# A fused attention and expert kernel: the first slots of its tail are put in another order

## The chip, the cores and the metric

The kernel runs on one core of a Trainium2 chip. The metric is device time in microseconds, the median of several runs; lower is better. Before the change it is 1239.16 us (three runs, 1238.08 to 1239.4). The five engines are named as the profile names them: PE (matrix products), DVE (vector), ACT (scalar, and a queue of DMA issues of its own), POOL (GpSimd, which also issues gathers and scatters) and SP (issues most DMAs).

## The reference, cut to what matters

```python
def _attn_ref(q, k, v):                      # 8 batches, 8 heads, 576 rows, 64 columns
    scores = scale * np.matmul(q, k.transpose(0, 1, 3, 2))
    kth = np.partition(scores, -32, axis=-1)[..., -32:-31]
    scores = np.where(scores >= kth, scores, -1e9)       # the 32 largest of each row stay
    attn = np.exp(scores - max); attn = attn / (sum(attn) + 1e-9)
    return np.matmul(attn, v)
def _moe_ref(x, w_gate, w_output_gate, w1, w2):          # x: 4608 rows of 512; 8 experts
    e_idx = np.argmax(x @ w_gate, axis=1)                # one expert for each row
    gate_w = softmax(x @ w_gate) at e_idx
    eom = 1.0 / (1.0 + np.exp(-(x @ w_output_gate)))
    for e in range(8):
        mask = e_idx == e
        h = np.maximum(x[mask] @ w1[e], 0.0)             # 512 to 1024
        out[mask] = gate_w * eom[mask, e] * (h @ w2[e])  # 1024 to 512
    return out
```

Everything is float32. The rows of `x` are the attention's output, so which expert a row goes to is known only when its attention is done.

## The kernel before

The attention runs over 36 tiles of 128 rows. 144 steps (a tile and a pair of heads each) form scores, find the 32nd largest, weigh and multiply with the values. Each finished tile is written to DRAM (`x_rows`), and gates its 128 rows. Tiles are collected in 12 groups. When a group's last tile is gated, `group_route` (L548) computes on DVE each row's expert and its place, and POOL scatters one list entry for each row into `ids` in DRAM (L612). Then a slot table is made (`slot_table`, L641): which expert's weights a slot of 128 rows takes and where its list begins.

A slot is the work for 128 rows of one expert: its list is read from `ids` by a DMA in ACT's queue (`fetch_id`, L743), its rows are gathered by POOL (`xg`, L759), turned on PE (L769) and copied by ACT (`xs`, L772); `up` is 64 products with the first weights `w1t` (L780), in two halves; `down` follows with the second weights `w2t`; `put` (L798) copies and scatters the result. Weights are 2 MB each, fetched by SP, with two buffers each.

During the attention, slots are woven between its steps (`heavy`). The tail is what follows the last step. Three slots belong to the last group but one: call them A, B and C. A is under way as the tail begins and its `down` pieces run in `while heavy`. B and C, and nine slots D to L of the last group, run in `slots_in_turn`. There `down` is done in three passes of faster products: `split` has ACT copy half of a slot's second weights to `w2h` (L1084) and DVE subtract that from them to `w2l` (L1085); `up_split` makes `hth` on ACT (L1092) and `htl` on DVE (L1093); `down_split` multiplies (L1102), 12 products for each half. `w2h`, `w2l`, `hth` and `htl` lie in a pool (`mp2`) that takes the memory of the attention's keys and scores.

Between these pieces `background` gates the last tile, routes the last group and issues its scatters; `last_table` makes the last slot table on DVE (L658 to L699), from which SP and ACT read weights' and lists' places (`last_slots`). `unsettled` (L189 to L203) is a check over all thresholds: eight operations on DVE, a small product on PE (L198) and four more on DVE, the last of which writes `more`; at the program's end all engines read `more` and jump past a spare path.

The program's order is the order in which this code issues instructions: each engine's queue is filled in that order, and nothing reorders it.

Of the kernel before, what the change touches and what calls it, by code (L numbers as in the profile page):

```python
# [10 lines left out]
F32 = mybir.dt.float32  # L11
F32R = mybir.dt.float32r
# [3 lines left out]
AF = mybir.ActivationFunctionType  # L16
ALU = mybir.AluOpType
# [6 lines left out]
P = 128  # L24
# [18 lines left out]
def tile_topk_attention_moe(  # L43
# [11 lines left out]
    nc = tc.nc  # L55
# [6 lines left out]
    NF = FF // P  # L62
# [120 lines left out]
    def unsettled(cp, pp):  # L183

        lo = cp.tile([P, 2], F32, name="lo")

        far = cp.tile([P, NTT * H], F32, name="gap")
        gap = far.rearrange("p (i a) -> p i a", a=2)
        nc.vector.tensor_scalar(gap, NEAR[:, :, :, 1], 1.0 + 2.0 ** -19, None, op0=ALU.mult)  # L189
        nc.vector.tensor_tensor(gap, gap, NEAR[:, :, :, 0], op=ALU.subtract)  # L190
        nc.vector.tensor_reduce(lo[:, 0:1], far, axis=AX.X, op=ALU.max)
        nc.vector.tensor_scalar(far, KTH, -1.0, None, op0=ALU.mult)
        nc.vector.tensor_tensor(far, far, KTH, op=ALU.max)
        nc.vector.tensor_reduce(lo[:, 1:2], far, axis=AX.X, op=ALU.min)
        nc.vector.tensor_scalar(lo[:, 0:1], lo[:, 0:1], 0.0, None, op0=ALU.is_ge)
        nc.vector.tensor_scalar(lo[:, 1:2], lo[:, 1:2], TINY, None, op0=ALU.is_le)
        bad = pp.tile([P, 2, P], F32, name="po")
        nc.tensor.matmul(bad[:1, 0, :2], ones[:, 0:1], lo, start=True, stop=True)  # L198
        total = cp.tile([1, 1], F32, name="total")
        nc.vector.tensor_reduce(total, bad[:1, 0, :2], axis=AX.X, op=ALU.add)  # L200
        nc.vector.tensor_copy(flag, total)
        nc.vector.tensor_tensor(total, total, over, op=ALU.add)
        nc.vector.tensor_copy(more, total)  # L203

    def run(exact, stack):
# [48 lines left out]
        def fill(n=1, single=False):  # L254
            for _ in range(n):
                if urgent:
                    urgent.popleft()()
                elif small and not (single and getattr(small[0], "two", False)) and small[0]() is not False:
                    small.popleft()
# [462 lines left out]
        W, G, XS, HT, PY = {}, {}, {}, {}, {}  # L722
        gathers = [0]
        tail = [False]

        def expert(g, k):
            if g in FIXED:
# [8 lines left out]
            W.setdefault(s, [None, None])[0] = a  # L736

        def fetch_w2(s, g, k, rows):
            b = mp.tile([P, NF, DM], F32, name="w2t", bufs=2)
            nc.sync.dma_start(b, w2[expert(g, k)].rearrange("o (c p) f -> p (o c) f", p=P))  # L740
            W.setdefault(s, [None, None])[1] = b

# [22 lines left out]
        def turn(s, pool, name):  # L765
            x = G[s][1]
            px = pool.tile([P, NC, P], F32, name=name)
            for c in range(NC):
                nc.tensor.transpose(px[:, c, :], x[:, c * P:(c + 1) * P], ident)  # L769
            def ev():  # L770
                XS[s] = mp.tile([P, NC, P], F32, name="xs", bufs=2)
                nc.scalar.activation(XS[s], px, AF.Copy)  # L772
            return ev

        def up_products(s, f0):
            w = W[s][0]
            ph = pools["p"].tile([P, 4, P], F32, name="pm")
            for f in range(f0, f0 + 4):
                for c in range(NC):
                    nc.tensor.matmul(ph[:, f - f0, :], w[:, c, f * P:(f + 1) * P], XS[s][:, c, :],  # L780
                                     start=(c == 0), stop=(c == NC - 1))
            return ph
# [44 lines left out]
        def ahead(what, f, n, after=None, lag=0):  # L827

            while had[what] < min(len(order), cur[0] + n):
                s = had[what]  # L830
                if after and when.get((after, s), clock[0]) + lag > clock[0]:
                    return
                f(s, *order[s])
                when[what, s] = clock[0]
                had[what] += 1
# [15 lines left out]
        def fetch_ahead():  # L851

            for what, f in (("w1", fetch_w1), ("w2", fetch_w2)):
                ahead(what, f, 1 if heavy else 2)
# [25 lines left out]
        def heavy_piece():  # L880

            return heavy.popleft()() if heavy else None
# [172 lines left out]
        def background():  # L1055
            step[0] += 1
            extra = side_start()
            if extra:
                extra(ps_t.tile([P, 4, P], F32, name="pst"))()
                side_use()  # L1060
            fill(60)
            run_slow(1e9, ("table", "done", "ids", "x", "out"))
# [2 lines left out]
        HL = {}  # L1065
        small_end = lambda: small.extend(slot_table(NGRP - 1, True) + [lambda: queue_slots(NGRP - 1, usual, N)])

        def slots_in_turn():

            def prepare(n):  # L1070
                ahead("id", fetch_id, min(n + 2, listed[0] - cur[0]))
                ahead("x", fetch_x, n + 1)
                ahead("w1", fetch_w1, n)
                ahead("w2", fetch_w2, n)

            def turned(n):
                ahead("turn", lambda s, *_: turn(s, pools["p"], "pm")(), min(n, had["x"] - cur[0]))

            def split(s, part):

                w = W[s][1][:, 4 * part:4 * part + 4]
                hi, lo = [pools["w"].tile([P, 4, DM], F32R, name=n, bufs=3) for n in ("w2h", "w2l")]
                HL[s, part] = hi, lo
                nc.scalar.activation(hi, w, AF.Copy)  # L1084
                nc.vector.tensor_tensor(lo, w, hi.bitcast(F32), op=ALU.subtract)  # L1085

            def up_split(s, f0):
                if f0 == 0:
                    HT[s] = [pools["w"].tile([P, NF, P], F32R, name=n, bufs=1) for n in ("hth", "htl")]
                ph = up_products(s, f0)  # L1090
                hi, lo = [x[:, f0:f0 + 4, :] for x in HT[s]]
                nc.scalar.activation(hi, ph, AF.Relu)  # L1092
                nc.vector.scalar_tensor_tensor(lo, ph, 0.0, hi.bitcast(F32), op0=ALU.max, op1=ALU.subtract)  # L1093

            def down_split(s, f0):
                if f0 == 0:
                    PY[s] = pools["p"].tile([P, DM], F32, name="pm")
                hh, hl = HT[s]
                wh, wl = HL.pop((s, f0 // 4))
                for f in range(f0, f0 + 4):  # L1100
                    for k, (h, w) in enumerate(((hh, wh), (hh, wl), (hl, wh))):
                        nc.tensor.matmul(PY[s], h[:, f, :], w[:, f - f0, :], start=(f == 0 and k == 0),  # L1102
                                         stop=(f == NF - 1 and k == 2))

            def splitted(s, part):
                if s < min(len(order), had["w2"]) and (s, part) not in HL:
                    split(s, part)
            while cur[0] < len(order):
                s = cur[0]
                prepare(1)  # L1110
                turned(1)
                prepare(2)
                splitted(s, 0)
                splitted(s, 1)
                ahead("w2", fetch_w2, 3)
                for f0 in (0, 4):
                    up_split(s, f0)
                    yield
                ahead("w1", fetch_w1, 3)
                for part in range(2):  # L1120
                    splitted(s + 1, part)
                    down_split(s, 4 * part)
                    if part == 0:
                        turned(2)
                    yield
                put(s)
                cur[0] += 1

        while heavy:
            background()  # L1130
            fetch_ahead()
            ev = heavy_piece()
            if ev:
                ev()
        usual = min(NLAST, USUAL)
        background()
        def last_table():
            nonlocal small_end
            if small_end and not (urgent or small or side):
                small_end()  # L1140
                small_end = None
                fill(60)
                ahead("id", fetch_id, min(3, listed[0] - cur[0]))
                ahead("x", fetch_x, 2)
        for n, _ in enumerate(slots_in_turn()):
            background()
            if n:
                last_table()
        while urgent or small or side or small_end:
            background()  # L1150
            last_table()
        if not exact:
            unsettled(st, ps_o)
        for _ in slots_in_turn():
            pass

        def extra_slots():

# [79 lines left out]
```

## Time and profile before

| what | value |
|---|---|
| median of three runs | 1239.16 us |
| the profiled execution's own time | 1241.63 us |
| its span in the profile | 1239.8 us |
| PE, DVE, ACT, POOL busy | 93%, 87%, 77%, 58% of the span |
| 1080.30 to 1231.29 us | slots B to L in the tail |
| granted clock of PE | 0.98 of full speed over the span |

Busy time of PE is modelled from the pipelined products, so it does not say that PE runs at its peak. In a timeline, a number in square brackets is the time that the engine had stood idle before that row, and what ended it. Times are microseconds from the span's start, unless a column says ns.

### The profile page before, as it was taken

To read this page: it belongs to the slowest core of one execution; us is meant where nothing else is said; L and a number is where in the kernel's file an instruction comes from. 1 tells how busy PE (TensorE), PEld (TensorE's weight loads), DVE (VectorE), ACT (ScalarE), POOL (GpSimd) and SP (SyncE) were. 2 spreads that over 40 slices of the span, in tenths; PEclk is the share of its full clock that TensorE was granted. 3 is DMA by queue.
4 is the path that set the end of the run, shared out by engine and by line. 5 is a ranking of instruction groups with operands and counts; after the bars stand their busy time and mean duration, and the time that the engine had idled before them with its cause. 6 is when DMAs were issued, how large, how long until landed. Compare 5 with 4: busy or idle time off the path is not lost.

```text
span 1239.8 us, 31208 instructions
## 1 busy us (share of the span) xinstructions
PE 1158.6 (93%) x9946; PEld 892.9 (72%) x9946; DVE 1074.5 (87%) x6148; ACT 948.5 (77%) x1892; POOL 713.7 (58%) x1191
## 2 busy tenths in 40 slices
PE   5777777899999999999999999999999999989997
PEld 3555555777777777777777777777777777779996
DVE  6999999899999999999999999999999998254443
ACT  5999998888788888887887878888888787334542
POOL 6667667555446584867567675477765486223121
PEclk7999998899999999999999999999999999999999
DMA  6301245077445629297555755566365426499990
GB/s 141 71 19 35 56 165 190 28 217 267 167 160 162 185 97 323 74 297 254 187 178 177 236 182 190 178 208 214 134 232 192 173 70 256 145 342 388 364 353 28
DMA packets 113726, 227.40 MB, mean 183 GB/s; under 512 B 19206, under 2 KB 37894, under 8 KB 112528
## 3 DMA queue, kind: packets, MB, share of 16 engines
q1 hardware_dynamic: 99712, 205.61, 49.1%
q0 software_dynamic: 7552, 18.96, 4.4%
q8 instruction: 81, 1.33, 0.4%
q10 hardware_dynamic: 6288, 0.74, 0.4%
q14 instruction: 93, 0.76, 0.2%
HBM read 206.68 MB, written 20.69 MB: 183 GB/s over the span
## 4 chain that ended last, share of the span: by engine, by line
PE 65%; DVE 17%; POOL 8%; issue 4%; ACT 3%; DMA 2%; ACTq 1%; POOLq 0%; SPq 0%
PE pm L780 19%; PE pm L795 12%; PE po L479 9%; PE ps L307 8%; PE pst L444 8%; DVE cand L334 5%; POOL w L372 5%; PE pm L1102 4%; DVE v L389 3%; DVE ep L418 2%; DVE cand L345 2%; DVE v L342 2%; DMA w2t<-in_w_dram 1%; ACT marks L369 1%; PE pst L500 1%
## 5 line engine op out<-in xcount | busy, mean ns | idle before, releaser
L372 POOL TENSOR_TENSOR w<-s,marks 128x576 f32<-128x576 f32 x288 | 363.4, 1283 | 253.3 <-DVE ep L418 119.9
L334 DVE MAX8 cand<-s 128x8 f32<-128x72 f32 x2304 | 323.9, 222 | 10.9 <-ACT s L315 10.7
L780 PE MATMUL pm<-xs,w1t 128*128 128x128 f32 x2560 | 299.1, 276 | 3.5 <-ACT xs L772 3.5
L780 PEld LDWEIGHTS pm<-xs,w1t 128*128 128x128 f32 x2560 | 293.5, 193 | 5.2 <-ACT xs L772 4.4
L444 PE MATMUL pst<-ident,ep 128*128 128x128 f32 x1296 | 218.9, 285 | 59.0 <-ACT ep L434 48.6
L369 ACT ACTIVATE marks<-s,v 128x576 int8<-128x576 f32 x288 | 221.0, 772 | 61.9 <-DVE v L342 35.9
L444 PEld LDWEIGHTS pst<-ident,ep 128*128 128x128 f32 x1296 | 147.5, 143 | 130.8 <-ACT ep L434 56.2
L389 DVE MAX8 v<-w 128x8 f32<-128x576 f32 x288 | 209.1, 753 | 32.9 <-POOL w L372 31.9
L455 ACT ACTIVATE pT<-pst 128x512 f32<-128x512 f32 (+1 forms) x432 | 201.6, 488 | 37.2 <-PE pst L500 32.1
L795 PE MATMUL pm<-w2t,ht 128*128 128x512 f32 x464 | 208.8, 593 | 0.0
L418 DVE SCALAR_TENSOR_TENSOR ep<-s,kth,ep 128x576 f32<-128x576 f32 x256 | 200.4, 816 | 0.0
L315 ACT ACTIVATE s<-ps 128x1152 f32<-128x1152 f32 (+1 forms) x145 | 163.3, 1127 | 45.0 <-PE ps L307 43.2
L384 ACT ACTIVATE ep<-s,v 128x576 f32<-128x576 f32 x256 | 186.2, 774 | 0.0
L307 PE MATMUL ps<-kst,qst 64*128 64x288 f32 (+1 forms) x1280 | 180.8, 431 | 5.1 <-ACT s L315 5.1
L479 PEld LDWEIGHTS po<-pT,v 128*64 128x64 f32 x3200 | 161.7, 139 | 24.3 <-issue 23.4
L479 PE MATMUL po<-pT,v 128*64 128x128 f32 (+1 forms) x3200 | 178.5, 268 | 0.0
L795 PEld LDWEIGHTS pm<-w2t,ht 128*128 128x128 f32 x464 | 83.6, 190 | 83.4 <-issue 83.4
L307 PEld LDWEIGHTS ps<-kst,qst 64*128 64x128 f32 (+1 forms) x1280 | 97.7, 177 | 46.5 <-issue 23.9
L342 DVE MAX8 v<-cand 128x8 f32<-128x16 f32 (+2 forms) x864 | 129.3, 191 | 0.0
L806 POOL DMA_INDIRECT out_dram<-y,idt x40 | 52.3, 1307 | 127.8 <-ACT y L802 96.4
L345 DVE MATCH_REPLACE8 cand<-v,cand 128x16 f32<-128x16 f32 (+1 forms) x576 | 95.3, 174 | 0.0
L358 POOL TENSOR_SCALAR v<-v 128x2 f32<-128x2 f32 x144 | 36.3, 252 | 86.2 <-DVE v L342 86.1
(172 smaller groups left out, 1259.2 us busy)
## 6 DMA issues: line engine op xcount, KB each, us to landing
w1t<-in_w_dram SPq DMA_DIRECT2D x40, 2048.0 KB, 9.2
w2t<-in_w_dram SPq DMA_DIRECT2D x40, 2048.0 KB, 9.8
x_rows<-xu SPq DMA_DIRECT2D x36, 256.0 KB, 2.1
qst<-in_qa_dram SPq DMA_DIRECT2D x70, 128.0 KB, 3.2
v<-in_va_dram SPq DMA_DIRECT2D x8, 1024.0 KB, 5.2
kst<-in_ka_dram SPq DMA_DIRECT2D x14, 576.0 KB, 12.4
v<-in_va_dram SPq DMA_DIRECT2D x16, 64.0 KB, 9.5
ids<-far SPq DMA_DIRECT2D x1, 678.0 KB
```

The lines of the kernel that those rows point to most:

```text
L307: nc.tensor.matmul(ps[qs, a, n, :288], Q[t][rows, hp, qs], K[b][rows, hp, cols], start=True, stop=True)
L334: nc.vector.max(out=c[:, 8 * g:8 * g + 8], in_=SC[i, a][:, g * GW:(g + 1) * GW])
L369: nc.scalar.activation(m.bitcast(I8).rearrange("p (s b) -> p s b", b=2)[:, :, 1], s, AF.Sign, bias=vs[:, a, PIVOT - 1:PIVOT], scale=-(1.0 ...
L372: x = nc.gpsimd.tensor_tensor(w, s, m, op=ALU.add)
L384: nc.scalar.activation(EP[i][:, a, :], SC[i, a], AF.Exp, bias=VV[i][0][:, a, 32:33], scale=SCALE)
L389: nc.vector.max(out=VV[i][0][:, a, 24:32], in_=SW[i][0][a])
L418: LAST[0] = nc.vector.scalar_tensor_tensor(e, SC.pop((i, a)), kth_col(i, a), e, op0=ALU.is_ge, op1=ALU.mult, accum_out=SM[t][:, 2 * hp + a ...
L444: nc.tensor.transpose(ps[:, c - c0, :], pt[:, c * P:(c + 1) * P], ident)
L455: nc.scalar.activation(x, ps[:, :n, :], AF.Copy)
L479: nc.tensor.matmul(po[a * 64:(a + 1) * 64, k, qs], lhs, rhs, start=half and not k and not m, stop=(c == 3 and k == 1 and m == len(TT[t]) - 1))
L780: nc.tensor.matmul(ph[:, f - f0, :], w[:, c, f * P:(f + 1) * P], XS[s][:, c, :], start=(c == 0), stop=(c == NC - 1))
L795: nc.tensor.matmul(PY[s], HT[s][:, f, :], w[:, f, :], start=(f == 0), stop=(f == NF - 1))
```

## The change

Five things change, all around the tail's beginning. (1) Of the second weights fetched in the tail, each third one, the first included, goes into a third buffer `w2x` in the pool `mp2`. (2) Before `while heavy` the tail now asks for the first and second weights of two slots ahead, and splits the first half of B's second weights; `fetch_ahead` in that loop is gone. (3) `last_table` is called before `slots_in_turn` begins. (4) `last_table` no longer reads lists or gathers rows; that is done in the loop, from its second piece on. `prepare`, at the head of a slot, reads lists too, as before. (5) `unsettled` is called as `settled()` from the ninth piece of `slots_in_turn`, instead of at the end. The functions inside `slots_in_turn` move out of it unchanged.

```diff
         def fetch_w2(s, g, k, rows):
-            b = mp.tile([P, NF, DM], F32, name="w2t", bufs=2)
+            if tail[0]:
+                thirds[0] += 1
+            if thirds[0] % 3 == 1:
+                b = pools["w"].tile([P, NF, DM], F32, name="w2x", bufs=1)
+            else:
+                b = mp.tile([P, NF, DM], F32, name="w2t", bufs=2)
...
+        sure = [exact]
+        def settled():
+            if not sure[0]:
+                sure[0] = True
+                unsettled(st, ps_o)
+        ahead("w1", fetch_w1, 2)
+        ahead("w2", fetch_w2, 2)
+        splitted(cur[0], 0)
         while heavy:
             background()
-            fetch_ahead()
             ev = heavy_piece()
...
                 small_end()
                 small_end = None
                 fill(60)
-                ahead("id", fetch_id, min(3, listed[0] - cur[0]))
-                ahead("x", fetch_x, 2)
+        background()
+        last_table()
         for n, _ in enumerate(slots_in_turn()):
             background()
-            if n:
-                last_table()
+            last_table()
+            if n and not small_end:
+                ahead("id", fetch_id, min(3, listed[0] - cur[0]))
+                ahead("x", fetch_x, 2)
+            if n >= 8 and not small_end:
+                settled()
         while urgent or small or side or small_end:
             background()
             last_table()
-        if not exact:
-            unsettled(st, ps_o)
         for _ in slots_in_turn():
             pass
+        settled()
```

What this does to the engines' order is seen at three places. On DVE, where the last tile is gated (`tl`) and the last group routed up to `oh1`, before:

```order
L545 RECIPROCAL r_16987<-r_16987 128x8
L535 TENSOR_TENSOR tl_17021<-pst_17016,r_16987 128x128
L537 TENSOR_REDUCE lg_15817<-tl_17021 128x16
L563 TENSOR_REDUCE mx_17024<-lg_15817 128x4
L564 TENSOR_TENSOR oh_17026<-lg_15817,mx_17024 128x32
```

And now:

```order
L545 RECIPROCAL r_16987<-r_16987 128x8
L1089 TENSOR_TENSOR w2l_17027<-w2t_16902,w2h_17026 128x2048
L535 TENSOR_TENSOR tl_17035<-pst_17030,r_16987 128x128
L537 TENSOR_REDUCE lg_15817<-tl_17035 128x16
L563 TENSOR_REDUCE mx_17038<-lg_15817 128x4
```

The subtraction of B's first half stands ahead of the gating; on ACT its copy (`w2h_17026`) stands in the same way ahead of the last tile's second copy `xu`.

On ACT, from B's splits to the next slot's, before (the list `idt_17175` is D's):

```order
L1084 ACTIVATE w2h_17091<-w2t_16902 128x2048
L1084 ACTIVATE w2h_17095<-w2t_16902 128x2048
L1092 ACTIVATE hth_17099<-pm_17101 128x512
L1092 ACTIVATE hth_17099<-pm_17120 128x512
L747 TENSOR_LOAD last_slots_99
L751 ISA
L751 DMA idt_17175<-ids_63 128x4
L1084 ACTIVATE w2h_17182<-w2t_17086 128x2048
```

And now, from A's result `y_17066` on (the lists are D's and E's, `w2h_17141` is B's second half, `hth_17150` B's):

```order
L808 ACTIVATE y_17066<-pm_16993,idt_16422 128x512
L753 TENSOR_LOAD last_slots_99
L757 ISA
L757 DMA idt_17131<-ids_63 128x4
L753 TENSOR_LOAD last_slots_99
L757 ISA
L757 DMA idt_17136<-ids_63 128x4
L1088 ACTIVATE w2h_17141<-w2t_16902 128x2048
L1096 ACTIVATE hth_17150<-pm_17152 128x512
L1096 ACTIVATE hth_17150<-pm_17171 128x512
```

The reading of the table and of two lists moved from behind B's `hth` to ahead of B's second split and of both `hth`. The first of these DMAs waits for the last of POOL's four scatters into `ids` (L612) to land, before and now.

On PE, the two halves of D's `up` with what follows, before:

```order
L780 MATMUL pm_17360<-xs_17321,w1t_17177 128x128 x16
L780 MATMUL pm_17379<-xs_17321,w1t_17177 128x128 x16
L1102 MATMUL pm_17407<-w2h_17299,hth_17358 128x512
L1102 MATMUL pm_17407<-w2l_17300,hth_17358 128x512
L1102 MATMUL pm_17407<-w2h_17299,htl_17359 128x512
```

And now:

```order
L786 MATMUL pm_17360<-xs_17321,w1t_17190 128x128 x16
L198 MATMUL po_17389<-lo_17379,ones_71 1x2
L786 MATMUL pm_17396<-xs_17321,w1t_17190 128x128 x16
L1106 MATMUL pm_17424<-w2h_17299,hth_17358 128x512
L1106 MATMUL pm_17424<-w2l_17300,hth_17358 128x512
```

The check's product stands between the halves; it reads `lo`, which DVE writes with eight operations that stand behind the `htl` of D's first half.

## Rows read from the trace of the kernel before

**Rows 1.** Busy time by stretch: time, PE, PEld, DVE, ACT, POOL, PEclk, DMA share, GB/s.
```profile
1097.30:1106.10 8.80, 8.80 (x65) 8.80 (x65) 4.73 (x3) 2.89 (x3) 4.47 (x4) 0.81 1.00 358
1126.50:1139.70 13.20, 13.20 (x94) 12.07 (x94) 6.04 (x5) 6.09 (x6) 3.00 (x3) 1.00 1.04 398
```

**Rows 2.** Timeline of PE: start, length, what; in brackets idle before and releaser.
```profile
1080.17 0.18 PE L582 MATMUL pst<-oh,before_b 128*128 128x40 bf16 x1
...
1097.27 9.04 PE L780 MATMUL pm<-xs,w1t 128*128 128x128 f32 x64 [3.45 <-ACT xs L772]
...
1109.83 0.66 PE L769 MATMUL pm<-ident,xg 128*128 128x128 f32 x4 [0.77 <-DMA xg<-x_rows,idt]
```

**Rows 3.** Chain of waits in the tail: start, time on the chain, what.
```profile
1120.74 2.77 PE pm L1102 x12
1123.51 0.44 PE pm L769 x4
...
1218.65 7.15 PE pm L780 x64
...
1231.29 0.13 PE po L198 x2
...
1231.98 0.15 DVE more L203
```

**Rows 4.** Timeline of ACT and of its DMA queue (ACTq) at the tail's beginning.
```profile
1076.93 0.38 ACT L503 ACTIVATE xu<-pst 128x256 f32<-128x256 f32 x1 [0.36 <-PE pst L500]
...
1080.37 0.69 ACT L802 ACTIVATE y<-pm,idt 128x512 f32<-128x512 f32 x1 [0.38 <-PE pm L795]
...
1087.73 0.60 ACT L1092 ACTIVATE hth<-pm 128x512 fp32r<-128x512 f32 x1 [2.58 <-PE pm L780]
1094.37 0.40 ACTq L751 DMA_DIRECT2D idt<-ids  x1
1094.82 1.91 ACT L1084 ACTIVATE w2h<-w2t 128x2048 fp32r<-128x2048 f32 x1 [6.49 <-DMA ids<-entry,posi]
1095.49 1.32 ACTq L751 DMA_DIRECT2D idt<-ids  x2
```

**Rows 5.** Timeline of DVE: gating, routing, split, table; the check at the end.
```profile
1077.35 0.29 DVE L535 TENSOR_TENSOR tl<-pst,r 128x128 f32<-128x128 f32 x1 [17.86 <-ACT xu L503]
...
1079.11 0.19 DVE L575 TENSOR_TENSOR oh<-first,fi 128x32 bf16<-128x32 f32 x1
...
1081.16 0.17 DVE L609 CAST posi<-pos 128x4 int32<-128x4 f32 x1
1082.89 4.49 DVE L1085 TENSOR_TENSOR w2l<-w2t,w2h 128x2048 fp32r<-128x2048 f32 x2 [1.56 <-ACT w2h L1084]
...
1088.96 0.15 DVE L658 TENSOR_TENSOR sl_cnt<-base,carry 1x8 f32<-1x8 f32 x1
...
1093.62 0.18 DVE L699 CAST last_slots<-sl_slot 1x50 int32<-1x50 f32 x1
...
1226.47 0.69 DVE L1093 SCALAR_TENSOR_TENSOR htl<-pm,hth 128x512 fp32r<-128x512 f32 x1 [2.88 <-ACT hth L1092]
...
1229.72 0.15 DVE L196 TENSOR_SCALAR lo<-lo 128x1 f32<-128x1 f32 x1
```

**Rows 6.** Timeline of POOL: the first two of four scatters of the last lists.
```profile
1082.71 0.96 POOL L612 DMA_INDIRECT ids<-entry,posi  x1 [0.22 <-issue]
...
1083.98 2.04 POOL L612 DMA_INDIRECT ids<-entry,posi  x1 [0.21 <-issue]
```

**Rows 7.** DMA issues, us to landing: scatters at 1019.94, 1004.12, 1083.98; `w2t` from 1000.
```profile
ids<-entry,posi POOLq DMA_INDIRECT x1, 2.3
...
ids<-entry,posi POOLq DMA_INDIRECT x1, 3.3
...
ids<-entry,posi POOLq DMA_INDIRECT x1, 7.1
...
w2t<-in_w_dram SPq DMA_DIRECT2D x12, 2048.0 KB, 10.8
```

More of the change, by code (lines that the diff above doesn't have):

```diff
@@ L724, in run @@
         tail = [False]
+        thirds = [0]
         def expert(g, k):
@@ L1066, in run @@
         small_end = lambda: small.extend(slot_table(NGRP - 1, True) + [lambda: queue_slots(NGRP - 1, usual, N)])
-        def slots_in_turn():
[L1070 to L1107, printed above, removed]
@@ new lines, in prepare, with turned, split @@
+        def prepare(n):
+            ahead("id", fetch_id, min(n + 2, listed[0] - cur[0]))
+            ahead("x", fetch_x, n + 1)
+            ahead("w1", fetch_w1, n)
+            ahead("w2", fetch_w2, n)
+        def turned(n):
+            ahead("turn", lambda s, *_: turn(s, pools["p"], "pm")(), min(n, had["x"] - cur[0]))
+        def split(s, part):
+            w = W[s][1][:, 4 * part:4 * part + 4]
+            hi, lo = [pools["w"].tile([P, 4, DM], F32R, name=n, bufs=3) for n in ("w2h", "w2l")]
+            HL[s, part] = hi, lo
+            nc.scalar.activation(hi, w, AF.Copy)
+            nc.vector.tensor_tensor(lo, w, hi.bitcast(F32), op=ALU.subtract)
@@ new lines, in up_split, with down_split @@
+        def up_split(s, f0):
+            if f0 == 0:
+                HT[s] = [pools["w"].tile([P, NF, P], F32R, name=n, bufs=1) for n in ("hth", "htl")]
+            ph = up_products(s, f0)
+            hi, lo = [x[:, f0:f0 + 4, :] for x in HT[s]]
+            nc.scalar.activation(hi, ph, AF.Relu)
+            nc.vector.scalar_tensor_tensor(lo, ph, 0.0, hi.bitcast(F32), op0=ALU.max, op1=ALU.subtract)
+        def down_split(s, f0):
+            if f0 == 0:
+                PY[s] = pools["p"].tile([P, DM], F32, name="pm")
+            hh, hl = HT[s]
+            wh, wl = HL.pop((s, f0 // 4))
+            for f in range(f0, f0 + 4):
+                for k, (h, w) in enumerate(((hh, wh), (hh, wl), (hl, wh))):
+                    nc.tensor.matmul(PY[s], h[:, f, :], w[:, f - f0, :], start=(f == 0 and k == 0),
+                                     stop=(f == NF - 1 and k == 2))
@@ L1108, in slots_in_turn, with splitted @@
+        def splitted(s, part):
+            if s < min(len(order), had["w2"]) and (s, part) not in HL:
+                split(s, part)
+        def slots_in_turn():
             while cur[0] < len(order):
@@ L1127, in slots_in_turn @@
                 cur[0] += 1
-        while heavy:
-            background()
-            fetch_ahead()
-            ev = heavy_piece()
-            if ev:
-                ev()
         usual = min(NLAST, USUAL)
-        background()
         def last_table():
@@ L1142, in last_table @@
                 fill(60)
+        sure = [exact]
[6 more added lines that the diff above has]
+        splitted(cur[0], 0)
+        while heavy:
+            background()
+            ev = heavy_piece()
+            if ev:
+                ev()
+        background()
+        last_table()
+        for n, _ in enumerate(slots_in_turn()):
+            background()
+            last_table()
+            if n and not small_end:
                 ahead("id", fetch_id, min(3, listed[0] - cur[0]))
                 ahead("x", fetch_x, 2)
-        for n, _ in enumerate(slots_in_turn()):
-            background()
-            if n:
-                last_table()
+            if n >= 8 and not small_end:
+                settled()
         while urgent or small or side or small_end:
```

## The prediction, made before the changed kernel ran

> **What bounds the kernel now.** I read four views, in this order. First the busy time by stretch: from slot D on PE never waits. In 1126.50 to 1139.70 it is busy 13.20 of 13.20 us at a clock of 1.00 [rows 1]. So in the tail every microsecond in which PE waits is a microsecond of the kernel, and nothing else counts. Then the timeline of PE for the waits that the tail does have: 3.45 us ahead of C's `up` at 1097.27, which waits for ACT's `xs`, and 0.77 us ahead of D's turn at 1109.83, which waits for a gather [rows 2]. After the first, the stretch 1097.30 to 1106.10 has a clock of 0.81: of 8.80 us, 0.19 or 1.67 us are lost, because part of it runs at 1.2 instead of 2.4 GHz [rows 1]. These three, 5.9 us, are all that a better order of the tail can win. Third, the chain of waits gives the lengths of a slot's pieces: 2.77 for half a `down`, 0.44 for a turn, 7.15 for an `up` [rows 3]; two halves, a turn and an `up` make a slot of 13.13. Fourth, the timelines of ACT, DVE and POOL show what would release PE in the new order.
>
> **Step 1, the split ahead of the gating.** ACT gets B's first copy ahead of the last tile's second `xu`. Before that `xu`, at 1076.93, ACT had been idle for 0.36 us [rows 4], so the copy begins at 1076.57, takes 1.91 [rows 4] and ends at 1078.48. DVE's subtraction, half of 4.49 or 2.25 [rows 5], stands ahead of `tl` and ends at 1080.73. `tl` began at 1077.35 [rows 5]; it moves by 3.38. All that hangs on it moves too: the one-hot choice `oh`, done at 1079.30 [rows 5], is done at 1082.68. PE's product over it (L582) ran at 1080.17 [rows 2], as soon as A's `down` was over. Now PE waits 2.51 us for it, and B's `up` begins as much later, at 1082.81, and ends 7.15 later at 1089.96. The 17.86 us in which DVE had nothing to do before `tl` [rows 5] are no cover, since the copy stands behind the last tile's `lt` on ACT.
>
> **Step 2, the lists ahead of the copies.** This is the large one. ACT now reads the last table and waits for D's list before it makes B's second copy and both `hth`. A wait of a DMA issue holds ACT: its copy at 1094.82 stood behind such an issue and ACT had been idle for 6.49 us, ended by the scatters' landing [rows 4]. So I need the time T at which the fourth scatter lands. A's result `y` cannot start before the exponent of the gate, which ended at 1079.99 (0.38 us before 1080.37 [rows 4]); with 3.38 more, `y` runs from 1083.37 and ends 3.00 later than before. The first scatter is behind `y`'s own on POOL: 1082.71 [rows 6] becomes 1085.71. Scatters follow each other at 1.27 us where none is slowed (1082.71 to 1083.98 [rows 6]), so the fourth starts at 1089.52. From issue to landing a scatter took 2.3, 3.3 and 7.1 us [rows 7]: the first with the DMA engines quiet, the last in the middle of 4 MB of weights. Here C's weights are asked for some ten microseconds earlier than before and are through, while D's have just been asked for; I take 3.3, T = 1092.8, and keep 1091.8 and 1096.6 as ends. The table itself does not hold ACT longer: its numbers end at 1081.33 (`posi`) plus at most 3.38, and it takes 4.84 (1088.96 to 1093.80) [rows 5], so 1089.6 at the latest.
>
> The second scatter of before took 2.04 us instead of 0.96 [rows 6], while DVE subtracted weights [rows 5]; I count all four at the short pace. The Trainium skill (SBUF — State Buffer, section "SBUF: two separate sides") has a reason for the long one: a DVE operation with two SBUF inputs and a GpSimd operation that reads SBUF exclude each other for a whole instruction. By that rule the new order, which has no subtraction beside the scatters, never sees the long pace; if two of the four stayed at 2.04, the sum below would be 2.16 more, 1253.8.
>
> The Trainium skill (DMA: Bandwidth & Descriptors, section "Anatomy of one DMA") gives 2.0 us plus the bytes over 436 GB/s for a transfer issued by GpSimd. By that estimate the 2 KB of a list land 1.3 us earlier than I count, and the sum would be 1250.3. No scatter of rows 7 is that quick, and the measured 2.3 to 7.1 decide.
>
> From T on, ACT issues the second list 0.92 later (two issues in 1.32, the first 0.40 long), and its engine follows 0.45 after an issue's start (1094.37 to 1094.82) [rows 4]: the copy runs from T+1.37 to T+3.28. `hth` takes 0.60 [rows 4], to T+3.88; DVE's second subtraction 2.25, to T+5.53, and behind it `htl` 0.69 [rows 5], to T+6.22. Of the 12 products of half a `down` two need no `htl`; the other ten take 2.31 of 2.77 us [rows 3] and end at T+8.53. A turn and the second half are 3.21: C's `up` begins at T+11.74 = 1104.56. Before, it began at 1097.27 [rows 2]. **Slot C starts 7.29 us later**, with PE idle for about 9 us from 1089.96 on, but for two products.
>
> **Step 3, what is saved.** Third buffer and early weights: D's second weights are asked for by 1090 and need some 10.8 us [rows 7], where D's `down` is 20 us away; the gather for D is issued right after T. So the 0.77 goes. The clock: a wait of 3.45 cost 1.67 us at the lower level before; the longer one costs at least as much, and up to twice that. I take the same 1.67, so nothing is saved there.
>
> **Step 4, the check.** PE's product for the check stands behind the first half of D's `up` and waits for `lo`. When PE ends that half, ACT makes `hth` (0.60), DVE `htl` and the eight operations, 3.40 from 1226.47 to the end of the last at 1229.87 [rows 5]. With 0.2 for hand-overs and the product, PE stands for 4.2 us. What is queued behind is the second half of `up`, so this is on the path in full. A wait of this length again costs clock: 1.67 as after the 3.45, with 0 as the lower end. What it saves at the end is almost nothing: between PE's last slot product and `more` lie 0.84 us (1231.29 to 1232.13 [rows 3]), but the last result's copy needs 0.69 of them anyway [rows 4]. I take 0, at most 0.15.
>
> **The sum.** 7.29 − 0.77 + 4.2 + 1.67 = 12.4. On the profiled execution: span 1239.8 + 12.4 = 1252.2, its own time 1.83 more, 1254.0; the median shown lies 2.47 below the profiled execution (1239.16 against 1241.63), so **1251.6**. Ends of the unknown costs: downwards −1.0 (T), −1.67 for each of two clock losses, −0.15 give 1247.1; upwards +3.8 (T), +1.67 for a longer loss after the 9 us and +1.67 after the wait of 2.51 give 1258.7.
>
> **Rivals.** (a) *ACT is not held*: if ACT's copies passed the waiting list, B's `down` would wait only for DVE, which has the second subtraction and `htl` behind the table: 1089.6 + 2.25 + 0.69 = 1092.5; C's `up` at 1092.5 + 2.31 + 3.21 = 1098.0, 0.8 later than before, with the first clock loss gone. 0.8 − 0.77 − 1.67 + 4.2 + 1.67 = 4.2: 1243.4. For it: on ACT the table came only at 1093.80, so part of the 6.49 us was another wait. Against it: the release is given to the scatters.
>
> (b) *The check costs nothing*: if DVE's eight operations lay in a wait that PE has anyway, 5.9 us fall away: 1245.7. But D's `up` comes 20 us after the long wait, and PE has no other.
>
> (c) *The lists land late*: D's weights start just as the scatters go out; at 7.1 us and with double the clock loss it is 12.4 + 3.8 + 1.67 = 17.9: 1257.1. The row of 7.1 speaks for it; that only two transfers are in flight, and young, speaks against.
>
> (d) *Not slower: the third buffer quickens the slots.* Its place is the ten slots C to L. The weights' transfers fill the DMA engines (share 1.04 [rows 1]); if they also slow PE's reading, asking earlier could shorten each slot. It decides from 1.24 us a slot on: a slot of 11.9 makes up for 12.4, and the time is 1239.2. Against: PE is busy in all of that stretch, and the last slot's `up`, with no weights coming in beside it, still takes 7.15 [rows 3].
>
> **How the numbers follow.** Forecast 0.69, (a) 0.07, (b) 0.05, (c) 0.11, (d) 0.08, half of that for more than it needs. A difference under 0.2% (2.5 us) is no change that this measurement could tell. All but (d) are slower: 0.92; same 0.04, faster 0.04. The range of 8 in 10 is 1245 to 1258: it leaves out (a) and (d), 0.15, and some 0.04 above.
>
> **What would show it.** After: L582 idle about 2.5 us with DVE as releaser; ACT without work from A's `y` to about 1093 and its copy released by the scatters; PE's first `down` product of B around 1097 and C's `up` around 1105 instead of 1097; L198 with some 4 us idle, released by DVE; then 13.13 a slot. It is wrong if ACT's copy for B runs before the lists land, or if slots take less than 13.

## The result

The changed kernel takes 1256.08 us (median of 4 runs, 1254.73 to 1258.37), the kernel before 1239.28 on the same chip. The ratio is 1.0138, 95% interval 1.0121 to 1.0156: **16.8 us slower**. The forecast was 1251.6, its range 1245 to 1258. The profiled execution took 1258.37 us, its span is 1256.6, and its granted clock over the whole span is 0.975.

### The profile page after: what moved, and what is told of

Same layout as the page of the kernel before. It is cut to its first block, busy times and chain, and to the rows that moved or that the text cites. A ratio compares the mean times of both kernels' runs of the same rounds, so it can differ in the third digit from the quotient of the medians.

```text
span 1256.6 us, 31210 instructions
## 1 busy us (share of the span) xinstructions
PE 1163.2 (93%) x9946; PEld 897.4 (71%) x9946; DVE 1073.6 (85%) x6148; ACT 948.7 (76%) x1892; POOL 710.8 (57%) x1191
## 4 chain that ended last, share of the span: by engine, by line
PE 57%; DVE 16%; issue 14%; POOL 10%; ACT 2%; DMA 2%; ACTq 0%; POOLq 0%
PE pm L786 14%; PE pm L801 13%; PE po L479 9%; PE ps L307 9%; PE pst L444 9%; POOL w L372 4%; DVE cand L334 4%; DVE v L389 3%; DVE ep L418 2%; DVE cand L345 2%; DVE v L342 2%; PE pst L500 1%; PE pst L775 1%; POOL xg L765 1%; ACT marks L369 1%
## 5 line engine op out<-in xcount | busy, mean ns | idle before, releaser
L786 PE MATMUL pm<-xs,w1t 128*128 128x128 f32 x2560 | 302.1, 278 | 0.0
L786 PEld LDWEIGHTS pm<-xs,w1t 128*128 128x128 f32 x2560 | 296.7, 194 | 1.0
```

## The profile after

In the changed file `up` is at L786 (it was L780), half a `down` at L1106 (L1102), a turn at L775 (L769), the copies for a split at L1088 (L1084); L582, L198 and the scatter L612 keep their numbers. The trace of after starts its tail some 0.4 us later than that of before; lengths below are taken from one trace each.

The busy time by stretch, the answer to [rows 1]; the columns are as there:

```profile
1083.10:1092.20 9.10, 9.09 (x69) 8.89 (x69) 5.29 (x37) 0.78 (x2) 5.40 (x9) 0.81 0.21 60
1092.20:1101.50 9.30, 0.00 (x0) 0.00 (x0) 0.49 (x1) 2.43 (x3) 0.00 (x0) 0.62 0.98 370
1101.50:1111.40 9.90, 8.66 (x28) 6.50 (x29) 5.30 (x5) 4.66 (x4) 1.12 (x2) 0.67 0.89 314
1128.40:1132.50 4.10, 0.08 (x2) 0.09 (x2) 3.23 (x9) 0.53 (x1) 0.62 (x2) 0.93 1.04 395
1132.50:1139.30 6.80, 6.80 (x35) 6.77 (x35) 0.58 (x4) 0.00 (x0) 0.00 (x0) 0.54 0.07 24
```

The second row is the loss: 9.30 us in which PE does nothing, in a tail where it had no wait over 3.45. The fourth is the second loss, 4.1 us. The third and the fifth follow those waits and have clocks of 0.67 and 0.54: there PE works, largely at 1.2 instead of 2.4 GHz.

PE's timeline, the answer to [rows 2]; the bracket at a row's end is the idle time before it and its releaser:

```profile
1083.04 0.18 PE L582 MATMUL pst<-oh,before_b 128*128 128x40 bf16 x1 [2.27 <-ACT ex L569]
...
1083.17 9.02 PE L786 MATMUL pm<-xs,w1t 128*128 128x128 f32 x64
1101.52 0.80 PE L1106 MATMUL pm<-w2h,hth 128*128 128x512 f32 x1 [9.33 <-ACT hth L1096]
...
1103.96 0.80 PE L1106 MATMUL pm<-w2h,htl 128*128 128x512 f32 x1 [1.22 <-DVE htl L1097]
...
1111.43 7.31 PE L786 MATMUL pm<-xs,w1t 128*128 128x128 f32 x64
...
1121.35 0.60 PE L775 MATMUL pm<-ident,xg 128*128 128x128 f32 x4
...
1124.56 3.74 PE L786 MATMUL pm<-xs,w1t 128*128 128x128 f32 x32
...
1132.42 0.19 PE L198 MATMUL po<-lo,ones 128*1 128x2 f32 x2 [4.12 <-DVE lo L196]
1132.54 6.78 PE L786 MATMUL pm<-xs,w1t 128*128 128x128 f32 x32
...
1145.14 7.31 PE L786 MATMUL pm<-xs,w1t 128*128 128x128 f32 x64
...
1158.28 7.31 PE L786 MATMUL pm<-xs,w1t 128*128 128x128 f32 x64
```

The rows in order: the gating's product waits 2.27 us; B's `up`; B's `down` waits 9.33 for ACT's `hth` and 1.22 for DVE's `htl`; C's `up` at 1111.43; D's turn, which no longer waits for its gather; the first half of D's `up`; the check's product with its 4.12; the second half of D's `up`, which takes 6.78 where the first took 3.74; and the `up` of E and of F. So slot C takes 13.13 us, D 20.58, E 13.14 again. From the gating's product to C's `up` it is 28.39 us; before, it was 17.10 (1080.17 to 1097.27 [rows 2]).

ACT's timeline says what held `hth`, the answer to [rows 4]:

```profile
1097.81 1.22 ACTq L757 DMA_DIRECT2D idt<-ids  x2
1099.07 1.91 ACT L1088 ACTIVATE w2h<-w2t 128x2048 fp32r<-128x2048 f32 x1 [14.91 <-issue]
1100.89 1.07 ACT L1096 ACTIVATE hth<-pm 128x512 fp32r<-128x512 f32 x2
```

ACT did nothing for 14.91 us, and its first row then is the issue of the two lists. The chain of waits names what that issue waited for, and how long (start, length):

```profile
1089.76 8.03 DMA ids<-entry,posi
1097.81 5.69 DMA idt<-ids
```

The scatter of the fourth list is issued at 1089.76 and lands 8.03 us later. What else was under way shows in the queue of the weights, on SP's timeline:

```profile
1089.51 0.37 SPq L746 DMA_DIRECT2D w2t<-in_w_dram  x1
1092.22 0.37 SPq L736 DMA_DIRECT2D w1t<-in_w_dram  x1
```

and in the view of the DMA engines, here their busy share in tenths, and GB/s, in 40 slices of 0.25 us from 1085 to 1095:

```profile
DMA  0000798000000001000010000001991468999999
GB/s 0 0 0 0 279 410 344 17 0 5 3 0 0 0 0 8 0 0 0 0 8 0 0 0 0 0 8 8 66 74 33 180 262 328 344 369 385 418 401 418
```

D's second weights are asked for 0.25 us ahead of the fourth scatter, and from 1092 on packets fill the engines; before that only A's result, near 1086, had used them. The first three scatters were issued ahead of these weights, the fourth behind them.

## The experiments

Each ratio below is to the kernel before on the same chip, with its 95% interval.

**The check at the end again.** The two lines in the loop are taken out:

```
-            if n >= 8 and not small_end:
-                settled()
```

> The changed kernel with the check (eight operations of VectorE, PE's product for it, and what reads the result) at the end again, as in the kernel before; nothing else differs. Theory: both PE's wait of 4.12 us at that product and the slower second half of D's up (6.78 instead of 3.57, so 3.2) come from the check's place. Then 7.3 go: 1256.1 - 7.3 = 1248.8. Rival 1: the clock falls there for another reason, only the wait goes: 1252.0. Rival 2: the early check also shortened the end (from PE's last product to the span's end 8.5 us before, 6.7 now); then 1.8 of it come back: 1250.6.

1250.25 us, 1.0093 (1.0076 to 1.0110): 0.45% below the change, some 5.6 us. PE then has no wait in D. The 7.3 of the one profile is more than the profiles of four runs below with the same check lose there: the second half of D's `up`, 6.78 in it, takes 5.17 to 6.50 in theirs. That is 1.6 to 2.9 us over the 3.57 of an undisturbed half, beside the 4.1 of the wait. The first theory holds with that spread, or with something given back at the end (rival 2); the next run looks at that.

**The check in two pieces.** The eight operations stay behind the first half of D's `up`; the product comes two pieces later:

```
+            if n >= 8 and n != 9 and not small_end:
+                settled(False)
```

The first of the two calls issues DVE's operations, the second PE's product.

> The changed kernel with the check's eight operations of VectorE where they are (behind the first half of D's up) and PE's product with what follows it two pieces of a slot later, behind the first half of D's down. Theory: PE doesn't wait then, so the 7.3 us go as in the run with the check at the end: 1248.8. If the end is shorter because the check is known early (rival 2 of that run), this one keeps the short end and is 1.8 faster than that one; if not, the two agree. Rival: VectorE's eight operations, 2.8 us, push back the subtractions that D's down needs and PE waits there instead: 1251 to 1253.

1249.49 us, 1.0087 (1.0070 to 1.0104). By the times it can't be told from the run before. The end of the trace does tell them apart. GpSimd's last scatter on its timeline in the run with the check last (span 1248.5):

```profile
1241.32 0.97 POOL L812 DMA_INDIRECT out_dram<-y,idt  x1 [10.73 <-DVE more L203]
```

and in this one (span 1248.8):

```profile
1243.07 0.97 POOL L815 DMA_INDIRECT out_dram<-y,idt  x1 [10.74 <-ACT y L811]
```

From its start to the end of the span it is 7.2 us where the check is last and 5.7 where it is early. So an early check is worth about 1.5 us, if PE does not wait for it.

**The lists behind the copies.** Slot B no longer reads lists in `prepare` (`begun` is B's number); the loop does, from its third piece on:

```
-            ahead("id", fetch_id, min(n + 2, listed[0] - cur[0]))
-            ahead("x", fetch_x, n + 1)
+            if cur[0] > begun:
+                ahead("id", fetch_id, min(n + 2, listed[0] - cur[0]))
+            ahead("x", fetch_x, min(n + 1, had["id"] - cur[0]))
...
-            if n and not small_end:
+            if n >= 2 and not small_end:
```

> The changed kernel with the last group's lists read behind B's copies and C's xs on ScalarE's queue (from the third piece of slot B on) instead of ahead of them. The table and the scatters stay where they are. Theory: the wait for the lists, queued ahead of B's copies on ScalarE, is all that holds slot B. Then C's up begins at about 1098.3 instead of 1111.4: 13.1 less, 1243.0, if D's gather keeps up. It may not: the fourth list landed at 1097.8, its read took 5.7 and the gather 6.4 more, so D's turn, due at 1108.3, could wait some 2.4 us and lose 1.7 of clock: 1247. Rival: B's copies wait for something else too (the table or the second weights): C's up stays behind 1105, time over 1250.

1247.50 us, 1.0070 (1.0053 to 1.0087). PE's timeline:

```profile
1082.30 0.18 PE L582 MATMUL pst<-oh,before_b 128*128 128x40 bf16 x1 [2.27 <-ACT ex L569]
...
1096.65 7.31 PE L786 MATMUL pm<-xs,w1t 128*128 128x128 f32 x64
...
1111.20 1.09 PE L775 MATMUL pm<-ident,xg 128*128 128x128 f32 x4 [4.47 <-DMA xg<-x_rows,idt]
...
1124.04 5.47 PE L786 MATMUL pm<-xs,w1t 128*128 128x128 f32 x32
```

C's `up` follows the gating's product after 14.35 us instead of 28.39: ACT's place for the lists was the whole of B's delay, and the rival is out. But the list lands as late as before (8.30 us by this run's chain), its read and the gather follow, and D's turn waits 4.47 us. Of the 14.0 us won ahead of C, 5.6 come back behind it by the ratios (4.47 in that wait); I expected 4.1. The last row is the second half of D's `up`, 5.47 here.

**The lists on the weights' queue.** In the tail, SyncE reads the lists, in program order ahead of D's weights:

```
-                                    engines=[ACT], ...
-            nc.scalar.dma_start(it, ids[place, :])
+                                    engines=[SP if tail[0] else ACT], ...
+            (nc.sync if tail[0] else nc.scalar).dma_start(it, ids[place, :])
```

> The changed kernel with the tail's lists read through the queue that also asks for the weights (SyncE) instead of ScalarE's. The order on it is kept, so D's weights are asked for only when the lists have landed, and ScalarE is not held. Theory: the fourth list landed 8.03 us after its issue because D's weights, asked for at 1089.5 and 1092.2, filled the DMA engines. Without them it lands after 2 to 3.3 us, at 1092 to 1093, C's up begins at 1098.3, D's gather is early: 13.1 less, 1243.0. Rival: the scatter is that slow by itself; then the list lands at 1097.8 again, D's weights are asked for 8 us later than now and D's up or down waits for them some 2 to 8 us: 1245 to 1252.

1242.68 us, 1.0030 (1.0017 to 1.0042). The timeline of PE, POOL and SP, with the fourth scatter, the read of the lists and the two halves of D's `up`:

```profile
1086.75 2.22 POOL L612 DMA_INDIRECT ids<-entry,posi  x1 [0.23 <-issue]
...
1090.51 1.24 SPq L757 DMA_DIRECT2D idt<-ids  x2
...
1109.07 3.81 PE L786 MATMUL pm<-xs,w1t 128*128 128x128 f32 x32 [1.37 <-DMA w1t<-in_w_dram]
...
1117.12 6.50 PE L786 MATMUL pm<-xs,w1t 128*128 128x128 f32 x32
```

The read of the list is issued 3.76 us after the scatter's start, of which the scatter itself took 2.22; DVE subtracted B's second half beside it, for 2.27 us from 1085.86 on. The time is what the theory gave; what remains is the check and 1.37 us ahead of D's `up`, which waits for its first weights.

**Only the weights held back.** Here ACT reads the lists as in the change. One more read of D's list, into a tile that nobody uses, stands on the weights' queue:

```
+                if not held:
+                    held.append(mp.tile([P, 4], I32, name="idd", bufs=1))
...
+                    nc.sync.dma_start(held[0], ids[bass.ds(ov, P), :])
                 ahead("w2", fetch_w2, 3)
```

SP reads `ov`, the place of D's list, from the table.

> The changed kernel with one more read of D's list, into a tile that nobody uses, on the queue that asks for the weights, ahead of D's second weights: D's weights are then asked for only when the lists have landed. ScalarE reads the lists as before and is held as before. Theory: D's weights in flight are what makes the fourth list land after 8.03 us; without them it takes 2.9 to 3.8 (the two runs with the lists on SyncE's queue), T is 4.3 to 5.1 us earlier, C's up as much, and the time is 1251 to 1252, what the forecast said with its landing of 3.3. Rival: the landing is as late as it was, 1256.

1249.02 us, 1.0086 (1.0073 to 1.0100). The timeline of PE, POOL and SP: the gating's product, the fourth scatter, SP's two issues, the first `down` product of B, C's `up` and the second half of D's:

```profile
1080.49 0.18 PE L582 MATMUL pst<-oh,before_b 128*128 128x40 bf16 x1 [2.27 <-ACT ex L569]
...
1087.20 0.96 POOL L612 DMA_INDIRECT ids<-entry,posi  x1 [0.23 <-issue]
...
1089.75 0.35 SPq L1129 DMA_DIRECT2D idd<-ids  x1
1090.66 0.38 SPq L746 DMA_DIRECT2D w2t<-in_w_dram  x1
...
1093.53 0.80 PE L1106 MATMUL pm<-w2h,hth 128*128 128x512 f32 x1 [5.52 <-ACT hth L1096]
...
1103.42 7.30 PE L786 MATMUL pm<-xs,w1t 128*128 128x128 f32 x64
...
1124.48 5.17 PE L786 MATMUL pm<-xs,w1t 128*128 128x128 f32 x32
```

The DMA engines' busy share in 40 slices from 1082 to 1093 shows A's result near 1084, ahead of the fourth scatter, and stays near 0 from there until the list has landed:

```profile
DMA  0000059800100001000000001000000020191089
```

With the engines empty the list lands within 2.55 us (1087.20 to 1089.75) instead of 8.03, and C's `up` comes 22.93 us after the gating's product instead of 28.39. That is 5.46 us, all from the landing: nothing on ACT, PE or DVE was moved. By the ratios the run is 6.4 us under the change and some 2 under the 1251 to 1252 that I expected; the second half of D's `up`, 5.17 in this profile instead of 6.78, is part of that.

**PE kept busy ahead of the check.** 36 transposes of the identity stand ahead of the check's product:

```
         bad = pp.tile([P, 2, P], F32, name="po")
+        for _ in range(36):
+            nc.tensor.transpose(bad[:, 1, :], ident, ident)
```

> The changed kernel with 36 transposes of the identity on PE (0.11 us each, some 4 us) ahead of its product for the check, into a corner of that product's own tile: PE waits for the check as long as before but is busy meanwhile. Theory: of the 7.3 us of the check's place the wait's 4.1 stay and the slow second half of D's up (3.2 in the profile of the changed kernel, 1.9 to 2.9 in two others) goes, since PE stays at 2.4 GHz: 1253 to 1254. Rival: the clock falls in any case, or the transposes cost as much as they save: 1256.

1253.70 us, 1.0108 (1.0092 to 1.0123): some 3.7 us below the change. The stretches of the transposes and of the second half of D's `up`:

```profile
1127.30:1131.30 4.00, 3.80 (x37) 3.56 (x35) 3.23 (x9) 0.47 (x1) 0.56 (x2) 1.00 1.03 380
1131.40:1135.00 3.60, 3.60 (x35) 3.60 (x33) 0.58 (x4) 0.00 (x0) 0.00 (x0) 1.00 0.11 42
```

The clock is 1.00 throughout and D's second half takes 3.6 us instead of 6.8. The wait itself costs 4.1, the clock after it as much as 3.2.

**No split ahead of the gating.** One line is taken out, so both halves are split behind the lists:

```
-        splitted(cur[0], 0)
         while heavy:
```

> The changed kernel without the split of B's first half ahead of the gating; both halves are then split in the slot, behind the lists. Theory (step 1): PE's wait of 2.27 us at the gating's product goes and everything that hangs on the gating is 3.4 us earlier. But the lists stand ahead of two copies instead of one: with the landing as slow as now, T at 1094.4, two copies and two subtractions behind it, C's up begins some 14 us after T, at 1108.4 instead of 1111.4: 3 less, 1253. Rival: the landing depends on D's weights; these are asked for when the table is ready, 3.4 us earlier too, so nothing changes against the scatters, and T moves by the full 3.4; or T doesn't move, then 1256 to 1257, since B's second copy now costs 1.9 to 2.3 more.

1252.99 us, 1.0106 (1.0091 to 1.0122). The gating's product doesn't wait, the scatters are earlier, D's weights too, 0.46 us behind the fourth scatter, and this list takes 6.85 us. The timeline of POOL and SP:

```profile
1083.84 0.96 POOL L612 DMA_INDIRECT ids<-entry,posi  x1 [0.21 <-issue]
...
1084.30 0.70 SPq L746 DMA_DIRECT2D w2t<-in_w_dram  x1
```

So the weights hold a scatter up that was issued ahead of them too. The list has landed 4.0 us earlier, counted from the last tile's transpose. Two copies and two subtractions behind the list take most of that back in slot B: only 0.7 reach C's `up`, counted in the same way (33.95 us against 34.64). The second half of D's `up` is 1.3 shorter (5.47). By the ratios the run is 4.0 under the change; the other 2 have no place in the two profiles, and are about the width of the intervals. So the time is the 1253 that I expected, but not by the way I expected: that it agrees is luck.

**D's first weights first.** To the lists on SyncE's queue this adds the check at the end, the order of D's weights, and `xs` ahead of the next copies:

```
-                ahead("w2", fetch_w2, 3)
                 for f0 in (0, 4):
...
                 ahead("w1", fetch_w1, 3)
+                ahead("w2", fetch_w2, 3)
                 for part in range(2):
-                    splitted(s + 1, part)
                     down_split(s, 4 * part)
                     if part == 0:
                         turned(2)
+                    splitted(s + 1, part)
```

> The kernel with the lists on SyncE's queue, and the check at the end, D's first weights asked for ahead of its second, and a slot's xs ahead of the next one's copies on ScalarE. Theory: the wait of 1.37 us for D's first weights and the check's 6 to 7 us are all that was left of the loss there: 1242.7 - 6.5 - 1.4 = 1234.8, under the kernel before. Rival: the weights come at the rate of the DMA engines (share 1.0), so that what D gains its second weights or E's lose: PE waits in a slot instead, 1236 to 1238.

1237.85 us, 0.9980 (0.9971 to 0.9989). From C's `up` on, PE has no wait left. In its profile B's `up` takes 9.02 us after the wait of 2.27, as in the change; that is 1.6 of the 3 us by which the time lies above what I expected. More is lost at the end, which I had left out: with the check late it is 8.1 us from GpSimd's last scatter to the end of the span, where it was 6.0 in the run with the lists on SyncE's queue.

**And without the early split.** The line `splitted(cur[0], 0)` goes too, and B's second half is split behind the first half of its `up`.

> The same, without the split ahead of the gating, and with B's second half split behind the first half of B's up (VectorE: table, w2l, htl, w2l, htl). Theory (step 1): the wait of 2.27 us at the gating's product goes, the lists land 3.4 us earlier, and B's down waits for the subtractions instead, some 0.6 and 1.2 us: 0.5 to 2 us under the other run, 1233 to 1234.5. Rival: the subtractions are later than I count and B's down waits 2.3 us or more: the same time as the other run, or above.

1235.20 us, 0.9958 (0.9945 to 0.9972): 2.7 us below the run before by the ratios, where I expected 0.5 to 2. In place of the 2.27 us (and of a clock loss that can follow) PE waits once, 1.03 us, for DVE:

```profile
1087.12 0.49 PE L1106 MATMUL pm<-w2l,hth 128*128 128x512 f32 x1 [1.03 <-DVE w2l L1089]
```

**With the check in two pieces.** The edit of the second experiment on top.

> The fastest kernel so far (lists on SyncE's queue, D's first weights first, no split ahead of the gating) with the check begun behind the first half of D's up and PE's product for it two pieces later, instead of the whole check at the end. Theory: from GpSimd's last scatter to the span's end it is 7.2 to 7.5 us where the check comes last and 5.7 where it comes early, in the profiles so far; 1.5 less, 1233.7. Rival: the eight operations of VectorE delay D's down, or the end is the same: 1235.2 or more.

1232.77 us, 0.9951 (0.9938 to 0.9965), the fastest of all, 0.5% under the kernel before. GpSimd's last scatter without this edit (span 1233.4):

```profile
1225.32 0.97 POOL L812 DMA_INDIRECT out_dram<-y,idt  x1 [8.53 <-DVE more L203]
```

and with it (span 1231.0):

```profile
1225.06 0.97 POOL L815 DMA_INDIRECT out_dram<-y,idt  x1 [8.52 <-ACT y L811]
```

The end takes 5.9 us against 8.1. Slot D takes 13.43 instead of 13.13, so 0.3 goes to the check. By the times alone the two can't be told apart.

**Without the third buffer.** The kernel of 1235.20 with `if thirds[0] % 3 == 1` made `if False`.

> The fastest kernel so far without the third buffer for second weights. Theory: with a slot's first weights asked for ahead of its second, the second weights have no use for an earlier place: the same time, 1235.2. Rival: the third buffer lets E's weights be asked for early enough that PE doesn't wait in D or E; without it PE waits there 1 to 3 us, 1236 to 1238.

1236.38 us, 0.9978 (0.9968 to 0.9987): 2 thousandths slower by the ratio, with intervals that just overlap. That is the rival's size, but by another way than I named. The profiled execution, 1240.67 us, is the slowest of eleven (the fastest 1234.29), so its waits may be longer than the usual ones. PE's timeline in D's `down`:

```profile
1116.16 0.50 PE L1106 MATMUL pm<-w2h,hth 128*128 128x512 f32 x1 [0.82 <-ACT hth L1096]
...
1118.42 0.80 PE L1106 MATMUL pm<-w2h,htl 128*128 128x512 f32 x1 [1.53 <-DVE htl L1097]
```

PE waits 2.35 us. The chain has the reason: C's second weights are now asked for only at 1080.08, they are in flight while the lists are scattered, the fourth list takes 5.67 us (in the chain `ids<-entry,posi`), and D's weights, which wait for it on the same queue, come late. ACT's copies of them stand ahead of both of D's `hth` and hold them. So in this profile the third buffer is good for the lists; that it makes the kernel faster is likely, not shown beyond the noise.

## Why the prediction was right, and where its sizes were off

The side, the places and the mechanisms came out as predicted: the wait at L582, ACT held by the lists, D's 0.77 us gone, PE waiting at L198, 13.13 us a slot after that. The sum was 12.4 us and 16.8 were measured, because two terms were too small and one, which goes the other way, was missed.

**Step 1** was 2.51; it is 2.27, released by the gating's exponent on ACT, not by DVE as I had it. That it can cost clock was counted only as an upper end: B's `up` takes 9.02 after it in the change and in two other runs, 7.39 in five. In the change that is hidden behind the lists.

**Step 2, the landing, is the term that was mis-sized.** The issue was forecast at 1089.52 and came at 1089.76, and the scatters kept the short pace (0.96 to 1.04). But I took 3.3 us for the landing, with 1096.6 as the latest T, from a row of 7.1; it took 8.03, T was 1097.8. I had written that D's weights were young then and C's through. In the run that only holds D's weights back the list lands in 2.55, in those that keep them in flight in 6.85 to 8.30, so being young is no help. The row of 3.3 misled me. Its scatter, at 1004.12, met only the rest of one weight transfer; the busy share before, in 40 slices of 0.3 us from 1000 to 1012, falls to 0 some 2.5 us later:

```profile
DMA  6923989999999999999982000000000000000000
```

How a list stays behind in the engines for so long is not shown. From T to C's `up` I counted 11.74; it took 13.64, with PE's clock at 0.67 in that stretch. That loss of 1.9 replaces the 1.67 that C's `up` lost before [rows 1], as counted. Rival (c) had the landing right in kind, and its time of 1257.1 is nearer to the result than the forecast. Part of that is luck: the loss that it doubled to 3.34, behind the long wait, came out at 1.9, and it left out the dearer check and the shorter end as I did.

Rival (a) is out: ACT doesn't pass the list. Rival (b) is out: PE waits for the check in full. Rival (d) is out: the slots keep 13.13 us.

The Trainium skill (DMA: Bandwidth & Descriptors, section "Anatomy of one DMA") gives 2.0 us and the bytes over 436 GB/s for a transfer from GpSimd. The empty engines' 2.55 us come near it; the 8.03 beside weights does not, and the 1250.3 that I estimated from it fell short for the same reason as my own sum.

The Trainium skill (SBUF — State Buffer, section "SBUF: two separate sides") says that a DVE operation with two SBUF inputs and a GpSimd operation that reads SBUF exclude each other. The trace agrees at both ends: no scatter of the change has a subtraction beside it and all are short; with the lists on SyncE's queue the fourth has one and takes 2.22 us.

**Step 4** was 4.2 us of wait and 1.67 of clock. The wait is 4.12. The clock cost 3.2 in the profiled execution and 1.6 to 2.9 in four others; in the run with transposes, where PE is busy through the same wait, it is gone. And I gave the early check nothing at the end: it is worth 1.5 to 1.8 us there (from GpSimd's last scatter to the span's end 7.5 us before, 7.2 with the check put back, 5.7 in the change). PE's last product and `more` are 0.84 us apart, as I had it; what shortens the program's end beyond that was not traced.

Put together: landing 4.7 more, clock behind the check 1.5 more, the end 1.8 less; 12.4 + 4.7 + 1.5 − 1.8 = 16.8. The other terms of the tail move by 0.5 or less each and come to some 0.4 less together; the tail's start, 0.4 later in this trace, makes up for that.

## What to carry to other kernels

A wait on a queue is a wait for everything behind it: put a wait for a DMA on the queue whose next work is to come after that DMA anyway (here the weights' own), not on an engine that has copies to make (ACT stood still for 14.91 us here). Before a small transfer that something waits for, look at which large ones are asked for in the same microseconds, and order them behind it. A wait of PE is to be priced with the slower clock after it, and a check moved off the end has to be moved in two pieces.

## What the runs showed of the hardware

- A scatter of 2 KB lands 2.55 us after its issue with empty DMA engines and 8.03 with two weight transfers asked for around it; being issued only 0.25 us later than a 2 MB transfer is enough, and 0.46 us ahead of one it still took 6.85.
- After waits of 4.1 us PE's granted clock is about 0.54 over the next 6.8 us in one execution, and half a slot's `up` takes 5.2 to 6.8 us instead of 3.6 from run to run. After waits of 2.27 the loss comes in some executions only (9.02 or 7.39 for the same `up`).
- Two scalings of GpSimd (L522) took 3.01 us while DVE subtracted weights, 1.18 in the run of 1235.20, where it did not:

```profile
1079.16 3.01 POOL L522 TENSOR_TENSOR xu<-xu,r 128x256 f32<-128x256 f32 x2 [16.84 <-ACT xu L503]
```
